# A bf16 softmax tail, a split last load and a 64-byte pad in a low-rank attention decode kernel

## The chip, the cores and the metric

One core of one Trainium2 chip. The metric is the device time of the whole program in microseconds (us), as the median of several runs. A profile (one execution recorded by the hardware profiler) has a span about 2 us shorter than the device time (330.8 against 332.58 before); it runs from the first instruction to the end of the last.

## The reference, cut to what matters

```python
B, H, Sq, Skv, Dh, R = 1, 16, 1, 8192, 256, 16     # all inputs bf16
kp = einsum("rn,bhnd->bhrd", e_proj, k)            # 8192 rows of K reduced to 16
vp = einsum("rn,bhnd->bhrd", f_proj, v)            # the same for V
scores = einsum("bhqd,bhrd->bhqr", q, kp) * Dh ** -0.5
p = softmax(scores)
o = einsum("bhqr,bhrd->bhqd", p, vp)
```

K and V are 16 heads x 8192 x 256 x 2 bytes each, 134.2 MB together, and every byte is used once. Everything after the two projections is tiny: 16 scores per head.

## The kernel before

The sync engine (SP) issues K and V in 64 transfers of 2 MB (half a head each), alternating, into five buffers of each. A transfer puts 16 KB in each of 128 partitions. For each chunk the tensor engine (PE) does 32 matmuls, one per slot of 128 rows, into four groups of 32 partitions of PSUM (the `psum_tensor` tiles that its matmuls write to). At the end of a head a "tail" adds the four groups and computes the attention:

```python
def T1(hh): ...   # kpT_ps <- kp_sb, S : add the four groups and transpose, 2 matmuls, fp32
def T2(hh): ...   # sc_ps  <- qT_sb, kpT_sb : 16 scores, 2 matmuls, fp32
def T3(hh):       # pT_ps  <- p_rep, S : the probabilities from a row to a column, fp32
    pe.wait_ge(sem_dve, dv_idx(hh, 4))
    ...
def T4(hh): ...   # o_ps   <- PT4, vp_sb : one row of the output, fp32
...
# where the tail stands in PE's order: the last head's T1, T2, T3 follow its last K chunk
if hh == H - 1:
    tgt = (2 * CH * H - 2) if t < 3 else (2 * CH * H - 1)
else:
    tgt = 2 * CH * (hh + 1) - 1 + t * step
```

Between T2 and T3, the vector engine (DVE) takes the maximum and scales it, the scalar engine (ACT) takes the exponential and its sum, and DVE takes the reciprocal and writes the normalised row four times (`p_rep`):

```python
dv.reciprocal(rs_sb[0:1, 0:1], sum_sb[0:1, 0:1]).then_inc(sem_dv2, 1)
...
for g in range(G):
    ins = dv.tensor_scalar(p_rep[0:1, 32 * g:32 * g + R], e_sb[0:1, 0:R],
                           rs_sb[0:1, 0:1], None, ALU.mult)
```

In the last head the matmuls of the last V chunk stand behind T3 in PE's program, and T3 waits for the whole softmax. The trace before has PE take them in that order: T3 began at 324.42 us, when `p_rep` was written, and the V matmuls at 324.88, though their data had landed at 323.33.

## Time and profile before

332.76 us, median of 4 runs (332.58 to 332.86).

The page of the profile, cut to some of its parts: the span; the busy time of the engines; the DMA strip in tenths of 40 equal slices; queues with packets, MB and share; the chain that ended last; the load of K with us from issue to landing. q1 carries K and V; q8, "instruction" on the page, is read as the program being fetched (17 packets here, 9 in the kernel of section 5 that has about half the PE instructions). PEld is PE's loading of weights, SPq is SP issuing a transfer.

```profile
span 330.8 us, 4863 instructions
PE 159.2 (48%) x2244; PEld 103.3 (31%) x2244; DVE 40.5 (12%) x181; ACT 7.0 (2%) x33; POOL 8.9 (3%) x18
...
DMA  8999999999999999999999999999999999999960
...
q1 hardware_dynamic: 9248, 134.23, 96.1%
...
q8 instruction: 17, 0.28, 0.3%
...
DMA 89%; PE 7%; issue 2%; DVE 1%; POOL 0%; ACT 0%; ACTq 0%; DVEq 0%; POOLq 0%
...
kbuf<-in_k_dram SPq DMA_DIRECT2D x32, 2048.0 KB, 47.0
```

The kernel is bound by the DMA: at nine tenths from the second slice to the 38th of 40, no engine above half. A transfer takes 47.0 us from issue to landing, and one lands every 4.9 us in the landing records, so about ten are queued (estimate: 47.0 / 4.9). A wait of PE or DVE in the middle did not stop the stream: PE waited 149.4 us for K and V in all (72.2 and 77.2 on the page), and the strip stays at nine tenths. So the two places where time can be saved are the stream itself and the drain, which is the work left after the last data has landed.

The timeline of the drain (start us, duration us, engine, line, operation, what it writes and reads, count; in brackets how long the engine was idle, and for what):

```profile
318.49 1.90 PE L323 MATMUL kp_acc<-kbuf,Wk 128*32 128x256 bf16 x32 [2.37 <-DMA kbuf<-in_k_dram]
...
321.16 1.04 PE L245 MATMUL kpT_ps<-S,kp_sb 112*128 112x16 f32 x4
...
322.48 0.26 PE L258 MATMUL sc_ps<-kpT_sb,qT_sb 128*1 128x16 f32 x4 [0.28 <-DVE kpT_sb L361]
...
323.73 0.64 DVE L377 TENSOR_SCALAR p_rep<-e_sb,rs_sb 1x16 f32<-1x16 f32 x4
...
324.42 0.53 PE L269 MATMUL pT_ps<-S,p_rep 1*112 1x1 f32 x2 [1.68 <-DVE p_rep L377]
...
324.88 1.90 PE L323 MATMUL vp_acc<-vbuf,Wv 128*32 128x256 bf16 x32
326.90 0.42 DVE L388 COPY vp_sb<-vp_acc 128x256 f32<-128x256 f32 x1 [2.53 <-PE vp_acc L323]
...
327.44 1.03 PE L279 MATMUL o_ps<-vp_sb,PT 112*16 112x256 f32 x2 [0.67 <-DVE PT L392]
328.51 0.41 DVE L396 CAST out_sb<-o_ps 16x256 bf16<-16x256 f32 x1 [1.12 <-PE o_ps L279]
328.95 0.36 SPq L204 DMA_DIRECT2D out_dram<-out_sb  x1
```

The V matmuls start at 324.88, and the bracket that a DMA wait would leave is missing: they came straight after pT. The chunk they read had landed 1.5 us earlier. That can't be seen in this view; it is in the landing records of the trace. Each of the 64 transfers of K and V has sixteen of them. The page reckons with 16 DMA engines, so I read them as one per engine, here and below; the records do not name the engine. The sixteen of the last V chunk, in us from the start of the span:

```
318.75 318.77 318.88 318.89 318.90 318.99 319.07 320.98 321.97 321.99 322.01 322.14 322.16 322.19 322.20 323.33
```

Seven engines are done at 318.9, seven at 322.1, one in between, and one, alone, at 323.33. The program waits for all sixteen, so the transfer counts as landed at 323.33.

### The profile page before, as it was taken

To read this page: it belongs to the slowest core of one execution; us is meant where nothing else is said; L and a number is where in the kernel's file an instruction comes from. 1 tells how busy PE (TensorE), PEld (TensorE's weight loads), DVE (VectorE), ACT (ScalarE), POOL (GpSimd) and SP (SyncE) were. 2 spreads that over 40 slices of the span, in tenths; PEclk is the share of its full clock that TensorE was granted. 3 is DMA by queue.
4 is the path that set the end of the run, shared out by engine and by line. 5 is a ranking of instruction groups with operands and counts; after the bars stand their busy time and mean duration, and the time that the engine had idled before them with its cause. 6 is when DMAs were issued, how large, how long until landed. Compare 5 with 4: busy or idle time off the path is not lost.

```text
span 330.8 us, 4863 instructions
## 1 busy us (share of the span) xinstructions
PE 159.2 (48%) x2244; PEld 103.3 (31%) x2244; DVE 40.5 (12%) x181; ACT 7.0 (2%) x33; POOL 8.9 (3%) x18
## 2 busy tenths in 40 slices
PE   0164364455446455455445445455355446536364
PEld 0143242243233324233223233334233233324242
DVE  0420101010010100101010010100101010010102
ACT  1000000000000000000000000000000000000000
POOL 8200000000000000000000000000000000000000
PEclk9996555555555555555555555555555555555555
DMA  8999999999999999999999999999999999999960
GB/s 284 384 428 426 428 424 432 420 434 420 434 422 434 420 433 424 428 428 424 432 420 436 418 434 420 434 424 430 424 428 426 426 428 426 426 430 424 428 292 1
DMA packets 9459, 135.07 MB, mean 408 GB/s; under 512 B 1088, under 2 KB 1120, under 8 KB 1248
## 3 DMA queue, kind: packets, MB, share of 16 engines
q1 hardware_dynamic: 9248, 134.23, 96.1%
q0 software_dynamic: 192, 0.54, 0.5%
q8 instruction: 17, 0.28, 0.3%
q14 instruction: 2, 0.02, 0.0%
HBM read 134.75 MB, written 0.01 MB: 407 GB/s over the span
## 4 chain that ended last, share of the span: by engine, by line
DMA 89%; PE 7%; issue 2%; DVE 1%; POOL 0%; ACT 0%; ACTq 0%; DVEq 0%; POOLq 0%
DMA kbuf<-in_k_dram 86%; PE kp_acc L323 5%; DMA q_nat<-in_q_dram 3%; PE vp_acc L323 1%; PE o_ps L279 1%; POOL Wk_tmp L127 0%; PE kpT_ps L229 0%; PE kpT_ps L245 0%; DVE p_rep L377 0%; PE pT_ps L269 0%; DVE vp_sb L388 0%; DVE out_sb L396 0%; PE sc_ps L258 0%; ACT e_sb L214 0%; DVE kpT_sb L361 0%
## 5 line engine op out<-in xcount | busy, mean ns | idle before, releaser
L323 PE MATMUL kp_acc<-kbuf,Wk 128*32 128x256 bf16 x1024 | 60.7, 417 | 77.4 <-DMA kbuf<-in_k_dram 72.2
L323 PE MATMUL vp_acc<-vbuf,Wv 128*32 128x256 bf16 x1024 | 60.0, 413 | 77.2 <-DMA vbuf<-in_v_dram 77.2
L323 PEld LDWEIGHTS vp_acc<-vbuf,Wv 128*32 128x32 bf16 x1024 | 35.4, 138 | 101.8 <-DMA vbuf<-in_v_dram 92.1
L323 PEld LDWEIGHTS kp_acc<-kbuf,Wk 128*32 128x32 bf16 x1024 | 35.8, 139 | 90.2 <-DMA kbuf<-in_k_dram 75.1
L279 PE MATMUL o_ps<-vp_sb,PT 112*16 112x256 f32 x32 | 16.9, 633 | 0.7 <-DVE PT L392 0.7
L245 PEld LDWEIGHTS kpT_ps<-S,kp_sb 112*128 112x128 f32 x64 | 14.7, 320 | 6.8 <-issue 6.0
L245 PE MATMUL kpT_ps<-S,kp_sb 112*128 112x16 f32 x64 | 16.4, 377 | 0.0
L357 DVE COPY kp_sb<-kp_acc 128x256 f32<-128x256 f32 x16 | 6.8, 425 | 69.6 <-PE kp_acc L323 69.6
L361 DVE COPY kpT_sb<-kpT_ps 128x32 f32<-128x32 f32 x16 | 3.1, 192 | 80.7 <-PE kpT_ps L245 80.7
L214 ACT ACTIVATE e_sb<-sc_ps,nb_sb 1x16 f32<-1x16 f32 x16 | 4.3, 266 | 315.8 <-DVE nb_sb L369 315.8
L377 DVE TENSOR_SCALAR p_rep<-e_sb,rs_sb 1x16 f32<-1x16 f32 x64 | 10.2, 218 | 0.6
L365 DVE TENSOR_REDUCE m_sb<-sc_ps 1x1 f32<-1x16 f32 x16 | 2.6, 162 | 61.6 <-PE sc_ps L258 61.6
L269 PEld LDWEIGHTS pT_ps<-S,p_rep 1*112 1x112 f32 x32 | 7.1, 282 | 8.0 <-issue 6.2
L269 PE MATMUL pT_ps<-S,p_rep 1*112 1x1 f32 x32 | 8.5, 332 | 1.7 <-DVE p_rep L377 1.7
L392 DVE COPY PT<-pT_ps 112x1 f32<-112x1 f32 x16 | 2.5, 158 | 51.7 <-PE pT_ps L269 51.7
L229 PE MATMUL kpT_ps<-S,q_nat 16*128 16x16 f32 x4 | 1.0, 367 | 12.1 <-DMA q_nat<-in_q_dram 12.1
L388 DVE COPY vp_sb<-vp_acc 128x256 f32<-128x256 f32 x16 | 6.5, 406 | 2.5 <-PE vp_acc L323 2.5
L258 PEld LDWEIGHTS sc_ps<-kpT_sb,qT_sb 128*1 128x1 f32 x64 | 4.8, 104 | 2.5 <-DVE kpT_sb L361 0.4
L279 PEld LDWEIGHTS o_ps<-vp_sb,PT 112*16 112x16 f32 x32 | 4.6, 147 | 2.9 <-DVE PT L392 1.1
L258 PE MATMUL sc_ps<-kpT_sb,qT_sb 128*1 128x16 f32 x64 | 5.0, 199 | 0.3 <-DVE kpT_sb L361 0.3
L229 PEld LDWEIGHTS kpT_ps<-S,q_nat 16*128 16x128 f32 x4 | 0.9, 319 | 12.1 <-DVE S L342 12.1
L373 DVE RECIPROCAL rs_sb<-sum_sb 1x1 f32<-1x1 f32 x16 | 2.4, 151 | 6.8 <-ACT e_sb L214 6.8
(23 smaller groups left out, 21.1 us busy)
## 6 DMA issues: line engine op xcount, KB each, us to landing
kbuf<-in_k_dram SPq DMA_DIRECT2D x32, 2048.0 KB, 47.0
vbuf<-in_v_dram SPq DMA_DIRECT2D x32, 2048.0 KB, 47.0
Wk_tmp<-in_e_proj_dram POOLq DMA_DIRECT2D x1, 256.0 KB, 9.4
Wv_tmp<-in_f_proj_dram POOLq DMA_DIRECT2D x1, 256.0 KB, 12.8
q_nat<-in_q_dram POOLq DMA_DIRECT2D x1, 16.0 KB, 9.4
out_dram<-out_sb SPq DMA_DIRECT2D x1, 8.0 KB, 1.4
```

The lines of the kernel that those rows point to most:

```text
L214: act.activation(e_sb[0:1, 0:R], sc_ps[0:1, 0:R], ACTF.Exp, bias=nb_sb[0:1, 0:1], scale=SCALE, accum_out=sum_sb[0:1, 0:1],).then_inc(sem_a ...
L245: ins2 = pe.matmul(kpT_ps[0:P, c2 * R:(c2 + 1) * R], kp_sb[0:KP, c2 * P:(c2 + 1) * P], S[0:KP, 0:R], start=True, stop=True,)
L258: ins2 = pe.matmul(sc_ps[0:1, 0:R], qT_sb[0:P, c2 * H + hh:c2 * H + hh + 1], kpT_sb[0:P, c2 * R:(c2 + 1) * R], start=(c2 == 0), stop=(c2 = ...
L269: pe.matmul(pT_ps[0:KP, 0:1], p_rep[0:1, 0:KP], S[0:1, 0:1], start=True, stop=True,).then_inc(sem_pe_t, 1)
L279: pe.matmul(o_ps[0:16, 0:D], PT4[0:KP, 16 * hh:16 * hh + 16], vp_sb[0:KP, 0:D], start=(hh == 0), stop=(hh == H - 1),).then_inc(sem_pe_t, 1)
L323: ins = pe.matmul(acc[32 * g:32 * g + MW, 0:D], W[0:P, j, 0:MW], buf[0:P, s, 0:D], start=(j < G), stop=(j >= JT - G), tile_position=(0, 32 ...
L357: dv.tensor_copy(kp_sb[0:KA, 0:D], kp_acc[hh % 2][0:KA, 0:D]).then_inc(sem_dve, 1)
L361: dv.tensor_copy(kpT_sb[0:P, 0:2 * R], kpT_ps[0:P, 0:2 * R]).then_inc(sem_dve, 1)
L365: dv.tensor_reduce(m_sb[0:1, 0:1], sc_ps[0:1, 0:R], AX.X, ALU.max).then_inc(sem_dv2, 1)
L377: ins = dv.tensor_scalar(p_rep[0:1, 32 * g:32 * g + R], e_sb[0:1, 0:R], rs_sb[0:1, 0:1], None, ALU.mult,)
L388: dv.tensor_copy(vp_sb[0:KA, 0:D], vp_acc[hh % 2][0:KA, 0:D]).then_inc(sem_dve, 1)
L392: dv.tensor_copy(PT4[0:KP, 16 * hh + hh:16 * hh + hh + 1], pT_ps[0:KP, 0:1]).then_inc(sem_dve, 1)
```

## The change

The intent is to shorten the work behind the last K and V chunk. The tail becomes bf16, the normalisation moves from the 16 probabilities to the output (a column of ones in `vp_sb` yields the sum), exp writes its four copies itself, T3 of the last head moves behind the V matmuls, and the last V chunk comes in two transfers. A `pad` tile of 64 bytes is added ahead of the K and V buffers. The core of the diff:

```diff
-    NDV = 6
+    NDV = 5
...
-        kp_sb = ... [P, D], fp32        # also kpT_sb, qT_sb, S, PT4, e_sb
-        vp_sb = ... [P, D], fp32
+        kp_sb = ... [P, D], bf16
+        vp_sb = ... [P, D + 1], bf16
...
+        pad = ctx.enter_context(nc.sbuf_tensor("pad", [P, 16], fp32))
         kbufs = []
...
+                    elif c == NCH - 1 and SL >= 2:
+                        h1 = 3 * SL // 4
+                        eng.dma_start(vbufs[c % NB][:, 0:h1, :], src[:, 0:h1, :]).then_inc(sem_vdma[c % NB], 16)
+                        eng.dma_start(vbufs[c % NB][:, h1:SL, :], src[:, h1:SL, :]).then_inc(sem_vlast, 16)
...
-                        e_sb[0:1, 0:R], sc_ps[0:1, 0:R], ACTF.Exp, ..., accum_out=sum_sb[0:1, 0:1],
+                        e_sb[0:1, 0:G, 0:R], sc_ps[...].to_broadcast([1, G, R]), ACTF.Exp, ...
...
-                            tgt = (2 * CH * H - 2) if t < 3 else (2 * CH * H - 1)
+                            tgt = (2 * CH * H - 2) if t < 2 else (2 * CH * H - 1)
...
-                    dv.reciprocal(rs_sb ...)            # and the four p_rep scalings, per head
...
-                dv.tensor_copy(out_sb[0:H, 0:D], o_ps[0:H, 0:D])
+                dv.reciprocal(rs_all[0:16, 0:1], o_ps[0:16, D:D + 1])
+                dv.tensor_scalar(out_sb[0:H, 0:D], o_ps[0:H, 0:D], rs_all[0:H, 0:1], float(G), ALU.mult, ALU.mult)
```

More of the change, by code (lines that the diff above doesn't have):

```diff
@@ L49, in bass_standalone__low_rank_proj_linformer__decode_kernel @@
     assert D <= 256 and 2 * max(H, R) <= 32
-    NDV = 6
-    POOL_TOTAL = 7 + G
+    NDV = 5
+    POOL_TOTAL = 9 + G
     W_CAST = (W_ENG == "pool")
@@ L57, in dv_idx @@
         return DV0 + NDV * h + step
-    DVE_FINAL = DV0 + NDV * H + 1
+    DVE_FINAL = DV0 + NDV * H + 2
     def pt_idx(h, t):
@@ L77, in bass_standalone__low_rank_proj_linformer__decode_kernel @@
         sem_out = ctx.enter_context(nc.semaphore("sem_out"))
+        sem_vlast = ctx.enter_context(nc.semaphore("sem_vlast"))
         Wk = ctx.enter_context(nc.sbuf_tensor("Wk", [P, JT, MW], bf16))
@@ L81, in bass_standalone__low_rank_proj_linformer__decode_kernel @@
         Wv_tmp = ctx.enter_context(nc.sbuf_tensor("Wv_tmp", [P, R, JT], bf16))
-        kp_sb = ctx.enter_context(nc.sbuf_tensor("kp_sb", [P, D], fp32))
-        vp_sb = ctx.enter_context(nc.sbuf_tensor("vp_sb", [P, D], fp32))
-        kpT_sb = ctx.enter_context(nc.sbuf_tensor("kpT_sb", [P, 2 * R], fp32))
-        qT_sb = ctx.enter_context(nc.sbuf_tensor("qT_sb", [P, 2 * H], fp32))
-        S = ctx.enter_context(nc.sbuf_tensor("S", [P, R], fp32))
+        kp_sb = ctx.enter_context(nc.sbuf_tensor("kp_sb", [P, D], bf16))
+        vp_sb = ctx.enter_context(nc.sbuf_tensor("vp_sb", [P, D + 1], bf16))
+        kpT_sb = ctx.enter_context(nc.sbuf_tensor("kpT_sb", [P, 2 * R], bf16))
+        qT_sb = ctx.enter_context(nc.sbuf_tensor("qT_sb", [P, 2 * H], bf16))
+        S = ctx.enter_context(nc.sbuf_tensor("S", [P, R], bf16))
         q_dt = fp32 if W_CAST else bf16
@@ L89, in bass_standalone__low_rank_proj_linformer__decode_kernel @@
         S16 = ctx.enter_context(nc.sbuf_tensor("S16", [16, 16], q_dt))
-        e_sb = ctx.enter_context(nc.sbuf_tensor("e_sb", [1, R], fp32))
-        m_sb = ctx.enter_context(nc.sbuf_tensor("m_sb", [1, 1], fp32))
+        e_sb = ctx.enter_context(nc.sbuf_tensor("e_sb", [1, G, 32], bf16))
         nb_sb = ctx.enter_context(nc.sbuf_tensor("nb_sb", [1, 1], fp32))
-        sum_sb = ctx.enter_context(nc.sbuf_tensor("sum_sb", [1, 1], fp32))
-        rs_sb = ctx.enter_context(nc.sbuf_tensor("rs_sb", [1, 1], fp32))
-        p_rep = ctx.enter_context(nc.sbuf_tensor("p_rep", [1, P], fp32))
-        PT4 = ctx.enter_context(nc.sbuf_tensor("PT4", [P, H * 16], fp32))
+        rs_all = ctx.enter_context(nc.sbuf_tensor("rs_all", [16, 1], fp32))
+        PT4 = ctx.enter_context(nc.sbuf_tensor("PT4", [P, H * 16], bf16))
         out_sb = ctx.enter_context(nc.sbuf_tensor("out_sb", [H, D], bf16))
@@ L104, in bass_standalone__low_rank_proj_linformer__decode_kernel @@
         pT_ps = ctx.enter_context(nc.psum_tensor("pT_ps", [P, 1], fp32))
-        o_ps = ctx.enter_context(nc.psum_tensor("o_ps", [16, D], fp32))
+        o_ps = ctx.enter_context(nc.psum_tensor("o_ps", [16, D + 1], fp32))
+        pad = ctx.enter_context(nc.sbuf_tensor("pad", [P, 16], fp32))
         kbufs = []
@@ L146, in stream_dmas @@
                         )
+                    elif c == NCH - 1 and SL >= 2:
+                        h1 = 3 * SL // 4
+                        src = v_src(hh, ch)
+                        eng.dma_start(vbufs[c % NB][:, 0:h1, :], src[:, 0:h1, :]).then_inc(
+                            sem_vdma[c % NB], 16
+                        )
+                        eng.dma_start(vbufs[c % NB][:, h1:SL, :], src[:, h1:SL, :]).then_inc(
+                            sem_vlast, 16
+                        )
                     else:
@@ L177, in _ @@
                 gp.wait_ge(sem_pool, pc[0])
-                pstep(gp.memset(p_rep[:, :], 0.0))
+                pstep(gp.memset(vp_sb[0:KA, D:D + 1], 1.0))
+                gp.wait_ge(sem_pool, pc[0])
+                pstep(gp.memset(e_sb[:, :, :], 0.0))
+                gp.wait_ge(sem_pool, pc[0])
+                pstep(gp.memset(rs_all[:, :], 0.0))
                 gp.wait_ge(sem_pool, pc[0])
@@ L214, in _ @@
                     act.activation(
-                        e_sb[0:1, 0:R],
-                        sc_ps[0:1, 0:R],
+                        e_sb[0:1, 0:G, 0:R],
+                        sc_ps[0:1, 0:R].rearrange("p (g r) -> p g r", g=1).to_broadcast([1, G, R]),
                         ACTF.Exp,
                         bias=nb_sb[0:1, 0:1],
-                        scale=SCALE,
-                        accum_out=sum_sb[0:1, 0:1],
+                        scale=1.0,
                     ).then_inc(sem_act, 1)
@@ L267, in T3 @@
                 def T3(hh):
-                    pe.wait_ge(sem_dve, dv_idx(hh, 4))
-                    pe.matmul(
-                        pT_ps[0:KP, 0:1],
-                        p_rep[0:1, 0:KP],
+                    pe.wait_ge(sem_act, hh + 1)
+                    ins2 = pe.matmul(
+                        pT_ps[0:KA, 0:1],
+                        e_sb[0:1, :, :].rearrange("p g r -> p (g r)"),
                         S[0:1, 0:1],
@@ L274, in T3 @@
                         stop=True,
-                    ).then_inc(sem_pe_t, 1)
+                    )
+                    ins2.then_inc(sem_pe_t, 1)
                 def T4(hh):
-                    pe.wait_ge(sem_dve, dv_idx(hh, 6))
+                    pe.wait_ge(sem_dve, dv_idx(hh, 5))
                     pe.matmul(
-                        o_ps[0:16, 0:D],
+                        o_ps[0:16, 0:D + 1],
                         PT4[0:KP, 16 * hh:16 * hh + 16],
-                        vp_sb[0:KP, 0:D],
+                        vp_sb[0:KP, 0:D + 1],
                         start=(hh == 0),
@@ L317, in _ @@
                     if ch == 0 and hh >= 2:
-                        pe.wait_ge(sem_dve, dv_idx(hh - 2, 1 if pj == 0 else 5))
+                        pe.wait_ge(sem_dve, dv_idx(hh - 2, 1 if pj == 0 else 4))
                     ins = None
@@ L322, in _ @@
                         g = j % G
+                        if pj == 1 and c == NCH - 1 and SL >= 2 and s == 3 * SL // 4:
+                            pe.wait_ge(sem_vlast, 16)
                         ins = pe.matmul(
@@ L343, in _ @@
                 dv.wait_ge(sem_pe_t, 1)
-                dv.tensor_copy(qT_sb[0:P, 0:2 * H], kpT_ps[0:P, 0:2 * H]).then_inc(
-                    sem_dve, 1
-                )
+                dv.tensor_scalar(
+                    qT_sb[0:P, 0:2 * H], kpT_ps[0:P, 0:2 * H], SCALE, None, ALU.mult
+                ).then_inc(sem_dve, 1)
                 dv.wait_ge(sem_wk, 16)
@@ L365, in _ @@
                     dv.tensor_reduce(
-                        m_sb[0:1, 0:1], sc_ps[0:1, 0:R], AX.X, ALU.max
-                    ).then_inc(sem_dv2, 1)
-                    dv.wait_ge(sem_dv2, 2 * hh + 1)
-                    dv.tensor_scalar(
-                        nb_sb[0:1, 0:1], m_sb[0:1, 0:1], -SCALE, None, ALU.mult
-                    ).then_inc(sem_dve, 1)
-                    dv.wait_ge(sem_act, hh + 1)
-                    dv.reciprocal(rs_sb[0:1, 0:1], sum_sb[0:1, 0:1]).then_inc(sem_dv2, 1)
-                    dv.wait_ge(sem_dv2, 2 * hh + 2)
-                    ins = None
-                    for g in range(G):
-                        ins = dv.tensor_scalar(
-                            p_rep[0:1, 32 * g:32 * g + R],
-                            e_sb[0:1, 0:R],
-                            rs_sb[0:1, 0:1],
-                            None,
-                            ALU.mult,
-                        )
-                    ins.then_inc(sem_dve, 1)
+                        nb_sb[0:1, 0:1], sc_ps[0:1, 0:R], AX.X, ALU.max, negate=True
+                    ).then_inc(sem_dve, 1)
                     if hh >= 1:
@@ L395, in _ @@
                 dv.wait_ge(sem_pe_t, pt_idx(H - 1, 4))
-                dv.tensor_copy(out_sb[0:H, 0:D], o_ps[0:H, 0:D]).then_inc(sem_dve, 1)
+                dv.reciprocal(rs_all[0:16, 0:1], o_ps[0:16, D:D + 1]).then_inc(sem_dve, 1)
+                dv.wait_ge(sem_dve, DVE_FINAL - 1)
+                dv.tensor_scalar(
+                    out_sb[0:H, 0:D], o_ps[0:H, 0:D], rs_all[0:H, 0:1], float(G),
+                    ALU.mult, ALU.mult,
+                ).then_inc(sem_dve, 1)
 _INS = ['q', 'k', 'v', 'e_proj', 'f_proj']
```

## The prediction

> **What bounds it now.** The kernel reads 134.2 MB of K and V in 64 transfers of 2 MB. The 40-slice strip shows the DMA engines at 9 tenths from the second slice to the next to last, at about 427 GB/s; the chain of waits is 89% DMA. The page shows 47.0 us from issue to landing, so about ten transfers are always queued and no engine work in the middle holds the stream up. PE is busy 48% with a granted clock of 0.5, DVE 12%, ACT 2%. Work removed in the middle (heads 0 to 14) therefore saves nothing.
>
> What counts is the drain. In the timeline the last K chunk is waited for until 318.49 us. By the landing records of its semaphore the last V chunk lands at about 323.3 us (half of the engines are done at 318.8, most of the others at 322.0, one at 323.3). The span ends at 330.8. Its order: K matmuls 1.90, o_ps of head 14 0.84 more, kpT 1.0, copy 0.2, scores 0.28, max and bias 0.35, exp 0.27, reciprocal 0.16, four p_rep scalings 0.65, pT matmul 0.53, and only then (324.9) the V matmuls, 1.9, because PE runs in order and pT stands ahead of them. Then vp copy 0.42, PT 0.08, o_ps 1.05, cast 0.41, store about 1.9.
>
> **What changes there.**
> - PE no longer sits behind softmax: pT is moved behind the V matmuls. The fp32 matmuls become bf16; each fp32 one shows as two records now (o_ps 2 x 0.63 us overlapped into 1.05), so I estimate o_ps 0.4 (one 256-column bf16 matmul here shows 0.42), kpT 0.35. Scores should end near 321.6.
> - The last V chunk comes in 3/4 and 1/4. The slowest engine's last chunk takes 4.9 us from K's landing, so 3/4 should land near 322.1 and the rest at 323.3. V matmuls run from about 322.1 to 324.0 (now 324.9 to 326.8); max, exp run beside them.
> - Added at the end: pT after V (about 0.2, beside the 0.42 vp copy), PT copy 0.15 now exposed, reciprocal 0.15, and scaling instead of cast, about 0.41. o_ps falls by 0.65.
> Sum: 324.05 + 0.45 copy + 0.17 PT + 0.4 o_ps + 0.2 reciprocal + 0.45 scale + 1.9 store = about 327.6, or 3.2 us less. The extra Pool memsets at the start (some 0.1 to 0.3 us each) delay the first matmuls, which don't bind: ten transfers are queued.
>
> **The stream itself.** One side effect: smaller tiles plus the 64-byte `pad` move the K and V buffers. By the layout they start at 192 modulo 256 now and would start at 0 modulo 256 afterwards. [...] A 16 KB packet takes 613 ns here[...]
>
> **Time.** 329.1 us, range 326.2 to 330.3. Chances: faster by over 2% 0.15, within 2% 0.84, slower 0.01.
>
> **Signs.** Right: DMA still 9 everywhere, V matmuls of the last chunk starting near 322 with two DMA waits, about 4.3 us from last landing to end (7.5 now), 16 KB packets still 613 ns. Wrong: [...]last K landing moved by over 1 us; or pT waiting on exp behind V.
>
> **Risks.** The buffer move, the straggling DMA engine landing elsewhere, the split's second semaphore landing late.

The forecast's sum was 332.8 us less 3.2 for the drain less 0.5 for the moved buffers: 329.1 us. The 0.5 term was the author's guess.

## The result, and the profile after

326.15 us, median of 8 runs (325.96 to 326.27); before in the same rounds 332.86 us (13 runs). The ratio is 0.9798, with a 95% interval of 0.9789 to 0.9808. Ratios here are the mean time of one kernel's fast runs over that of the other's of the same rounds, so they are not quite the ratio of the quoted medians. The interval reaches over 0.98, so whether the gain is more than 2% is left unclear. The gain is 6.7 us; the prediction had 3.7.

The page after, the same parts (span, engines, DMA strip, queues, chain):

```profile
span 324.2 us, 4563 instructions
PE 129.6 (40%) x2148; PEld 81.4 (25%) x2148; DVE 26.2 (8%) x86; ACT 6.2 (2%) x17; POOL 9.1 (3%) x20
...
DMA  7999999999999999999999999999999999999992
...
q1 hardware_dynamic: 9392, 134.23, 97.4%
...
q8 instruction: 17, 0.28, 0.3%
...
DMA 94%; PE 4%; SPq 0%; DVE 0%; issue 0%
```

The timeline of the drain after:

```profile
315.07 1.90 PE L337 MATMUL kp_acc<-kbuf,Wk 128*32 128x256 bf16 x32 [2.83 <-DMA kbuf<-in_k_dram]
...
317.50 0.22 PE L256 MATMUL kpT_ps<-S,kp_sb 112*128 112x16 bf16 x2 [0.33 <-DVE kp_sb L371]
...
318.01 0.20 PE L269 MATMUL sc_ps<-kpT_sb,qT_sb 128*1 128x16 bf16 x2 [0.28 <-DVE kpT_sb L375]
...
318.44 0.30 ACT L226 ACTIVATE e_sb<-sc_ps,nb_sb 1x64 bf16<-1x64 f32 x1 [10.59 <-DVE nb_sb L379]
...
318.72 1.90 PE L337 MATMUL vp_acc<-vbuf,Wv 128*32 128x256 bf16 x32 [0.51 <-DMA vbuf<-in_v_dram]
319.95 0.18 PEld L337 LDWEIGHTS vp_acc<-vbuf,Wv 128*32 128x32 bf16 x8 [0.25 <-DMA vbuf<-in_v_dram]
...
320.55 0.18 PE L280 MATMUL pT_ps<-S,e_sb 1*128 1x1 bf16 x1
320.73 0.42 DVE L385 CAST vp_sb<-vp_acc 128x256 bf16<-128x256 f32 x1 [2.33 <-PE pT_ps L280]
...
321.28 0.38 PE L291 MATMUL o_ps<-vp_sb,PT 112*16 112x257 bf16 x1 [0.55 <-DVE PT L389]
321.70 0.16 DVE L393 RECIPROCAL rs_all<-o_ps 16x1 f32<-16x1 f32 x1 [0.47 <-PE o_ps L291]
321.89 0.47 DVE L395 TENSOR_SCALAR out_sb<-o_ps,rs_all 16x256 bf16<-16x256 f32 x1
322.39 0.36 SPq L216 DMA_DIRECT2D out_dram<-out_sb  x1
```

Two things are to be seen. V now waits twice for DMA (at 318.72 for three quarters, at 319.95 for the rest) and no longer for the softmax. And the last K chunk is taken up at 315.07 instead of 318.49: the stream before the drain, which the change was not about, is 3.4 us shorter.

All data of the last V chunk has landed at 323.33 before and at 319.91 after. So the 6.56 us between the two spans divide into

- the stream, up to the last landing: 323.33 - 319.91 = 3.42 us;
- the drain, from the last landing to the end: 7.47 before and 4.33 after, 3.14 us.

The drain is what the prediction said ("about 4.3 us from last landing to end (7.5 now)"). The stream is where the other half came from. The landing records of the last transfer (the last quarter of V), after:

```
316.58 316.67 316.75 316.80 316.83 316.88 316.98 317.68 319.66 319.69 319.72 319.83 319.84 319.86 319.88 319.91
```

The early half moved from 318.9 to 316.8, the late half from 322.1 to 319.8, and the one engine that came alone at 323.33 is gone. These are two different effects: some 2.1 to 2.3 us for everybody, and 1.1 us for the straggler. The next section takes them apart.

The packets of K and V in the two traces (durations of the 16 KB packets in ns, with how many took that long; the change has fewer of 16 KB because the last V chunk has smaller ones):

```
before: 611 x476, 612 x710, 613 x4122, 614 x223, 615 x144, 616 x43, 618 x467, 620 x1644, 621 x73 ...   mean of those under 700 ns: 615.1
after:  611 x7768, 612 x14, 614 x18, 615 x14 ...                                             mean of those under 700 ns: 611.5
```

3.65 ns x 512 packets per DMA engine (8192 packets over 16 engines) = 1.9 us. The packets themselves became faster and uniform.

### The profile page after: what moved, and what is told of

Its sections match the earlier page's. It is cut to its first block, busy times and chain, and to the rows that moved or that the text cites. A ratio compares the mean times of both kernels' runs of the same rounds, so it can differ in the third digit from the quotient of the medians.

```text
span 324.2 us, 4563 instructions
## 1 busy us (share of the span) xinstructions
PE 129.6 (40%) x2148; PEld 81.4 (25%) x2148; DVE 26.2 (8%) x86; ACT 6.2 (2%) x17; POOL 9.1 (3%) x20
## 4 chain that ended last, share of the span: by engine, by line
DMA 94%; PE 4%; SPq 0%; DVE 0%; issue 0%
DMA vbuf<-in_v_dram 94%; PE vp_acc L337 4%; SPq L143 0%; DVE out_sb L395 0%; DVE vp_sb L385 0%; SPq L156 0%; PE o_ps L291 0%; DVE rs_all L393 0%; PE pT_ps L280 0%; DVE PT L389 0%
## 5 line engine op out<-in xcount | busy, mean ns | idle before, releaser
L371 DVE CAST kp_sb<-kp_acc 128x256 bf16<-128x256 f32 x16 | 6.8, 425 | 74.6 <-PE kp_acc L337 74.6
L226 ACT ACTIVATE e_sb<-sc_ps,nb_sb 1x64 bf16<-1x64 f32 x16 | 4.9, 305 | 311.8 <-DVE nb_sb L379 311.8
L375 DVE CAST kpT_sb<-kpT_ps 128x32 bf16<-128x32 f32 x16 | 3.1, 192 | 66.8 <-PE kpT_ps L256 66.8
L379 DVE TENSOR_REDUCE nb_sb<-sc_ps 1x1 f32<-1x16 f32 x16 | 2.6, 163 | 71.0 <-PE sc_ps L269 71.0
L291 PE MATMUL o_ps<-vp_sb,PT 112*16 112x257 bf16 x16 | 6.7, 420 | 0.6 <-DVE PT L389 0.6
L385 DVE CAST vp_sb<-vp_acc 128x256 bf16<-128x256 f32 x16 | 6.6, 413 | 2.7 <-PE pT_ps L280 2.3
L269 PEld LDWEIGHTS sc_ps<-kpT_sb,qT_sb 128*1 128x1 bf16 x32 | 3.9, 125 | 2.5 <-DVE kpT_sb L375 0.4
L269 PE MATMUL sc_ps<-kpT_sb,qT_sb 128*1 128x16 bf16 x32 | 3.9, 195 | 0.3 <-DVE kpT_sb L375 0.3
L256 PE MATMUL kpT_ps<-S,kp_sb 112*128 112x16 bf16 x32 | 3.5, 184 | 0.3 <-DVE kp_sb L371 0.3
L280 PE MATMUL pT_ps<-S,e_sb 1*128 1x1 bf16 x16 | 2.9, 180 | 0.0
```

The source lines that it names most:

```text
L226: act.activation(e_sb[0:1, 0:G, 0:R], sc_ps[0:1, 0:R].rearrange("p (g r) -> p g r", g=1).to_broadcast([1, G, R]), ACTF.Exp, bias=nb_sb[0:1 ...
L256: ins2 = pe.matmul(kpT_ps[0:P, c2 * R:(c2 + 1) * R], kp_sb[0:KP, c2 * P:(c2 + 1) * P], S[0:KP, 0:R], start=True, stop=True,)
L269: ins2 = pe.matmul(sc_ps[0:1, 0:R], qT_sb[0:P, c2 * H + hh:c2 * H + hh + 1], kpT_sb[0:P, c2 * R:(c2 + 1) * R], start=(c2 == 0), stop=(c2 = ...
L280: ins2 = pe.matmul(pT_ps[0:KA, 0:1], e_sb[0:1, :, :].rearrange("p g r -> p (g r)"), S[0:1, 0:1], start=True, stop=True,)
L291: pe.matmul(o_ps[0:16, 0:D + 1], PT4[0:KP, 16 * hh:16 * hh + 16], vp_sb[0:KP, 0:D + 1], start=(hh == 0), stop=(hh == H - 1),).then_inc(sem ...
L371: dv.tensor_copy(kp_sb[0:KA, 0:D], kp_acc[hh % 2][0:KA, 0:D]).then_inc(sem_dve, 1)
```

## The experiments

The theory after the result: (a) the drain gain is the shorter chain and the split; (b) the packets are faster because the K and V buffers start at a multiple of 256 bytes (192 modulo 256 before, 0 after, by the layout of the program); (c) the straggler went because the PE program is shorter and its last instruction fetch falls later. The rival to (b) and (c): the stream is faster because the engines do lighter work. For (c) the page has the first hint: q8 moved 17 packets of 16 KB, of the kind "instruction". In the kernel after, PE executed 201 to 270 instructions between two of them (256 on average), and one such packet took 0.89 to 1.27 us.

The table sums up what the traces of all runs say. It is worked out from packet and landing records: mean of the 16 KB packets of K and V under 700 ns, number of fetches, start of the last fetch, landing of the last V data in the early half (median of the first 7 engines), in the late half (median of the 9th to 15th) and of the last engine, and the drain from there to the end.

```
kernel                        time us  packet ns  fetches  last fetch  early   late    last    drain
before                        332.86   615.1      17       311.6       318.9   322.1   323.33  7.47
after                         326.15   611.5      17       319.7       316.8   319.8   319.91  4.33
before + pad                  330.54   611.4      17       309.3       316.8   319.6   321.43  7.53
after, no pad (offset 192)    328.54   615.1      17       322.0       318.9   322.1   322.29  4.31
after, offset 64              328.55   615.1      17       322.1       318.9   322.0   322.16  4.31
after, offset 128             328.43   614.9      17       322.1       318.9   321.8   322.17  4.32
after, V not split            327.19   611.5      17       320.9       316.7   319.6   319.90  5.57
after, pT before V            326.33   611.5      17       319.7       316.8   319.7   319.87  4.56
before, pT behind V           331.41   615.1      17       312.0       318.9   322.0   323.73  6.01
after, tail in fp32           328.61   611.4      17       309.6       316.6   319.7   321.16  5.55
after, PE instructions added  327.64   611.4      17       309.2       316.7   319.6   321.34  4.34
after, two slots per matmul   326.04   611.5       9       312.5       316.8   318.2   319.78  4.34
the same, fewer (wrong)       324.64   611.4       8       308.5       316.8   318.2   318.41  4.36
```

### 1. The pad alone, and the change without it

```diff
 (kernel before)
+        pad = ctx.enter_context(nc.sbuf_tensor("pad", [P, 16], fp32))
         kbufs = []
```
```diff
 (kernel after)
-        pad = ctx.enter_context(nc.sbuf_tensor("pad", [P, 16], fp32))
```

> The kernel before with one unused 64-byte tile in front of the K and V buffers, so that they start at 0 instead of 192 modulo 256; every instruction is as before. Alignment theory: 16 KB packets take 611 ns throughout (before: 613, with 620 in about 29 percent of them), about 2.0 us come off the stream, and the straggling engine at the last landing stays, because the instruction stream is unchanged: about 330.7 us. If alignment is the whole stream gain: about 329.4 us. Rival (the stream got shorter through the lighter bf16 engine work or fewer instructions): packets stay at 613 and 620 ns and the time stays at 332.8 us.

> The changed kernel without its pad tile: K and V buffers start at 192 modulo 256 again, as in the kernel before. Alignment theory: packets back at 613 and 620 ns, about 2.0 us more, 328.2 us. If alignment was the whole stream gain of 3.4 us: 329.5 us. Rival (lighter engine work): stays at 326.2 us with 611 ns packets.

Measured: 330.54 us (before in the same rounds 332.93, ratio 0.9931, interval 0.9916 to 0.9946), and 328.54 us (ratio 0.9870, interval 0.9853 to 0.9886). The pad is worth 2.39 us on the kernel before and 2.39 us on the kernel after. Not one instruction differs in the first pair, and packets go from 615.1 to 611.4 ns on average. In the second pair they go back to 615.1 although all engine work is the lighter kind. The rival is out for this part. In the padded kernel before one engine still lands alone (321.43 against a late half at 319.6): alignment did not remove the straggler. Of the 2.39 us, 1.9 are the packets under 700 ns. In the first pair the traces leave no rest: their spans differ by 1.85 us (330.80 and 328.95; the executions profiled were the fastest of the kernel before and the slowest of the padded one). In the second pair the spans differ by 2.36 us. A part of that rest is in the program fetches of section 5: with the slow packet behind it, one takes 1.56 us of an engine's time at offset 192 and 1.43 when aligned (medians). What is left beyond that was not looked into.

### 2. Is it the distance from 256 bytes?

```diff
-        pad = ctx.enter_context(nc.sbuf_tensor("pad", [P, 16], fp32))
+        pad = ctx.enter_context(nc.sbuf_tensor("pad", [P, 32], fp32))     # buffers at 64 modulo 256; [P, 48]: at 128
```

> The changed kernel with the buffers starting at 64 modulo 256. [...] If any misalignment to 256 costs the same: 328.2 us. If only 64-byte alignment matters: 326.2 us.

> The changed kernel with the buffers starting at 128 modulo 256. [...] If any misalignment to 256 costs the same: 328.2 us. If 128-byte alignment is what matters: 326.2 us and 611 ns.

Measured: 328.55 us at offset 64 and 328.43 us at offset 128, against 328.54 at 192 and 326.15 at 0. A buffer off by 64, 128 or 192 bytes costs the same, 2.3 to 2.4 us, and the packets take 614.9 to 615.1 ns at all three, against 611.5. The cost does not grow with the offset here. Smaller offsets were not tried.

### 3. The parts of the drain

The last V chunk in one transfer, with the rest of the change as it is:

```diff
-                    elif c == NCH - 1 and SL >= 2:
+                    elif False:
...
-                        if pj == 1 and c == NCH - 1 and SL >= 2 and s == 3 * SL // 4:
+                        if False:
```

> The changed kernel with the last V chunk in one transfer, as before. The last landing stays at 319.9 us in the trace; the 32 V matmuls can then start only there, and their 1.9 us stand whole behind it, instead of ending at 320.6: about 1.2 us more, 327.4 us. Rival (the split is worth nothing, because PE or the exp is what V waits for): 326.2 us.

Measured: 327.19 us (327.05 to 328.32), 1.04 us more. In its timeline the V matmuls start when everything has landed (319.90), and the store is issued 1.23 us later than in the kernel after:

```profile
319.95 1.90 PE L337 MATMUL vp_acc<-vbuf,Wv 128*32 128x256 bf16 x32 [1.68 <-DMA vbuf<-in_v_dram]
...
323.62 0.36 SPq L216 DMA_DIRECT2D out_dram<-out_sb  x1
```

The order of pT, put back in the kernel after, and changed alone in the kernel before:

```diff
 (kernel after)
-                            tgt = (2 * CH * H - 2) if t < 2 else (2 * CH * H - 1)
+                            tgt = (2 * CH * H - 2) if t < 3 else (2 * CH * H - 1)
```
```diff
 (kernel before)
-                            tgt = (2 * CH * H - 2) if t < 3 else (2 * CH * H - 1)
+                            tgt = (2 * CH * H - 2) if t < 2 else (2 * CH * H - 1)
```

> The changed kernel with pT of the last head ahead of the V matmuls in PE's order, as before. In the changed kernel exp ends at 318.74 us and V begins at 318.72, so pT would be in the way for only 0.2 us: 326.3 us. Rival (the order is a main part of the gain in the drain, as the prediction had it first in its list): 327.5 us or more.

> The kernel before with only the order changed: pT of the last head after the V matmuls. V should start when its chunk lands (323.4 us in the trace) instead of at 324.9, and pT and the PT copy then stand behind it: about 1.4 us less, 331.4 us. If the order is worth as little here as it should be in the changed kernel: 332.7 us.

Measured: 326.33 us (0.18 more than after, hardly beyond the spread of the runs, but the drain in its trace is 0.23 longer) and 331.41 us (1.4 less than before, 332.82 in the same rounds). The same edit is worth 1.4 us in one kernel and 0.2 in the other, because in the kernel after exp ends (318.74) just as V's data comes (318.72): the parts of the drain overlap, and their values can't be added. The moved normalisation and exp's four copies were not tested alone. In the kernel before with only the order changed, the bracket of the missing DMA wait appears:

```profile
323.77 1.90 PE L323 MATMUL vp_acc<-vbuf,Wv 128*32 128x256 bf16 x32 [0.62 <-DMA vbuf<-in_v_dram]
```

The small tiles and the tail matmuls in fp32 again, in the kernel after (the pad made larger so that the buffers stay at 0 modulo 256):

```diff
-        kp_sb = ... bf16      # and vp_sb, kpT_sb, qT_sb, S, e_sb, PT4
+        kp_sb = ... fp32
-        pad = ctx.enter_context(nc.sbuf_tensor("pad", [P, 16], fp32))
+        pad = ctx.enter_context(nc.sbuf_tensor("pad", [P, 40], fp32))
```

> The changed kernel with its small tiles and tail matmuls in fp32 again (buffers still at 0 modulo 256). The drain gets longer by o_ps 0.65, pT 0.35 and the V matmuls starting about 0.9 later, about 1.9 us; and the PE program again has the 12 more instructions per head, so an engine of the DMA should again straggle by about 1.1 us at the last landing. Together about 329.0 us; with the drain alone (no straggler): 328.0 us.

Measured: 328.61 us, 2.46 more. The table divides it: the last engine lands 1.25 us later (321.16), again alone, and the drain is 1.22 us longer (5.55). The drain part is smaller than the 1.9 expected: the straggler makes the last K chunk late too (taken up at 316.36), and V, which now waits for the scores and not for its data, starts 4.03 us after it, against 3.65 in the kernel after. The slower scores cost 0.4 and not 0.9. Each fp32 tail matmul stands in the trace as two, as in the kernel before; that is the link to the next experiment.

### 4. The straggler: as many PE instructions as before, without fp32

```diff
-                    for c2 in range(2):                                         # T1, the same in T2
+                    for c2 in (range(2) if hh == H - 1 else (0, 1, 0, 1)):
...
+                    for _rep in range(1 if hh == H - 1 else 3):                 # around the matmul of T3
```

> The changed kernel, with six of the bf16 tail matmuls of each head but the last simply repeated (same operands, same result), so that PE has as many instructions per head as in the kernel before (12 more). Instruction-fetch theory: the 17th 16 KB instruction fetch, which came at the very end in the changed kernel, comes back some 10 us before the end, one DMA engine gets a third one and lands its last share 1.1 to 1.5 us after all others: 327.4 us, with 611 ns packets and an unchanged drain of 4.3 us. Rival (the straggler came from fp32 or from the old buffer addresses): 326.2 us and no straggler.

Measured: 327.64 us, 1.49 more than after, with 611.4 ns packets and a drain of 4.34. Repeating 90 tiny matmuls whose own time is hidden behind the loads costs 1.5 us. The DMA view of the stretch from 307 to 318 us shows the reason. First the kernel before, then the kernel after, then this one (packets, MB, share of 16 engines; the share is lower in the last two because seven of their engines are done by 317 us):

```profile
q1 hardware_dynamic: 317, 4.62, 99.3%
q8 instruction: 1, 0.02, 0.6%
```

```profile
q1 hardware_dynamic: 386, 4.34, 92.6%
```

```profile
q1 hardware_dynamic: 388, 4.30, 92.0%
q8 instruction: 1, 0.02, 0.5%
```

The kernels with the long PE program fetch their 17th packet at 309 to 312 us, while data is still being moved; the short one fetches it at 319.7, when the data is practically there. And the last V data then lands at

```
with PE instructions added: 316.54 316.56 316.63 316.66 316.68 316.88 316.94 317.50 319.49 319.51 319.55 319.60 319.63 319.72 319.79 321.34
```

which is the list of the kernel after with one engine 1.55 us behind the others.

### 5. Where the two halves come from, and a shorter program

The landing lists of the kernel after can be read from its start to its end: how many of the sixteen engines land late in a transfer, against the median of the five earliest, and how many 16 KB program packets (q8) had begun by then.

```
transfer landed at (us)        9    32   51   70   90   109  129  148  168  189  208  227  247  266  286  305  320
program packets by then        0    1    2    3    4    5    6    7    8    9    10   11   12   14   15   16   17
engines over 1.1 us late       0    1    2    3    4    5    6    7    8    8    8    8    8    8    8    8    8
of them over 2.2 us late       0    0    0    0    0    0    0    0    0    1    2    3    4    5    6    7    8
```

By these counts one more engine is late after each fetch (for the first the slowest landing is 1.7 us behind the median at 32 us, for the ninth 3.2 us at 174 us, so about 1.5 us a fetch), and it stays behind to the end of the stream. The lateness falls on eight of the sixteen, once each with the first eight fetches and a second time with the next eight; the other eight are never over 1.1 us late. A fetch that began less than a microsecond before the landing does not show yet: the 14th, 15th and 16th in the columns of 266, 286 and 305 us, and the 17th, which began at 319.7 us and was too late to matter. So the late half, 3.0 us behind, is read as eight engines with two fetches each.

The packets show what the 1.5 us consist of, though their records name no engine. From 1 to 16 ns before each fetch ends, one 16 KB data packet begins that takes 1.07 to 1.16 us instead of 0.61. It is so for all 17 fetches of the kernel before and for 16 of the 17 of the kernel after, and in the other runs too, except for the last fetch of the kernels that fetch it as the data ends (319.7 us or later). In the kernels before and after no other 16 KB packet later than 16 us takes over 0.66 us, but for those behind q14 packets, named under what stays open. The fetch takes 0.88 to 1.11 us; with what the packet takes beyond 611 ns that is 1.42 to 1.58 us. And the durations of the slow packets repeat after eight fetches (kernel after, ns, in order of time):

```
1079 1079 1089 1158 1158 1102 1107 1114
1079 1079 1091 1158 1158 1102 1106 1115
```

The test is a kernel with half the PE instructions, two slots per matmul for all heads but the last:

```diff
-                    for s in range(SL): ...
+                    if hh < H - 1:
+                        for s in range(0, SL, 2):
+                            j = ch * SL + s
+                            g = (j // 2) % 2
+                            ins = pe.matmul(acc[64 * g:64 * g + 64, 0:2 * D],          # 64 x 512, diagonal blocks used
+                                W[0:P, j:j + 2, 0:MW].rearrange("p a r -> p (a r)"),
+                                buf[0:P, s:s + 2, 0:D].rearrange("p a d -> p (a d)"),
+                                start=(j < 4), stop=(j >= JT - 4), tile_position=(0, 64 * g), ...)
... (PSUM accumulators [P, 2 * D]; kp_sb and vp_sb evicted in four copies of 32 partitions)
```

> The changed kernel with two slots of a chunk per matmul for all heads but the last: 64 weight columns and 512 moving columns, of which the diagonal blocks are used, evicted in four copies. PE has about half the instructions. Instruction-fetch theory: about 9 fetches in place of 17; eight DMA engines that now end 3.0 us late (two fetches of about 1.5 us each) end 1.5 us late, so the stream ends 1.5 us sooner: 324.6 us (326.1 if the ninth still falls before the end). [...] Rival (the late half of the DMA engines is late for another reason than instruction fetches): 326.2 us with the same 3.0 us gap.

Measured: 326.04 us, correct, no better than the kernel after (ratios to before 0.9793 and 0.9798). PE takes 3.26 us for such a chunk (V at 298.92 us in its timeline), less than the 4.9 us between two landings in the kernel after. Its page (engines, queue of the program):

```profile
PE 181.9 (56%) x1188; PEld 74.7 (23%) x1188; DVE 63.9 (20%) x176; ACT 6.2 (2%) x17; POOL 9.1 (3%) x20
...
q8 instruction: 9, 0.15, 0.2%
```

The time alone would have been taken for "no effect". The landings say otherwise: the late half is now only 1.4 us behind the early one (318.2 against 316.8; 3.0 in the kernel after), and a single engine lands at 319.78. By the same count as above, eight engines are over 1.1 us late and one of them over 2.2: nine fetches fit one for each of eight engines and a second for one. It was foreseen as the second case in the expectation. To see what the ninth alone costs, the program was shortened further by leaving work out; the result is wrong.

```diff
-                        for s in range(0, SL, 2):
+                        for s in range(0, SL - 8 if ch == 0 and hh < H - 2 else SL, 2):
```

> WRONG RESULT ON PURPOSE, to size one thing: the two-slots-per-matmul kernel with the last 4 of 16 matmuls left out in the first chunk of K and of V of heads 0 to 13 (112 matmuls and weight loads fewer, all loads of K and V as before). PE waits for DMA anyway, so its work itself is worth nothing. Instruction-fetch theory: PE's program is some 220 instructions shorter, so the ninth fetch no longer falls before the end; no engine straggles, the last landing comes about 1.5 us sooner (at 318.3 us) and the time is 324.5 us. Rival (the straggler or the late half has another cause): 326.0 us, as the kernel with all its matmuls.

Measured: 324.64 us (ratio 0.9751, interval 0.9735 to 0.9768), last landing 318.41, eight fetches (queue of the program, from its page):

```profile
q8 instruction: 8, 0.13, 0.1%
```

So the theory's number came out again: with the ninth fetch inside the stream (at 312.5 us) the time is 1.4 us longer than with eight. One late engine is enough for that, as the program waits for all sixteen. A correct kernel at 324.6 us would need about 110 PE instructions fewer ahead of its last V chunk than the two-slots kernel has (estimate from the instruction counts in the traces: the last V chunk begins after about 2340 PE instructions, the ninth fetch came after 2266 here and after 2230 in the kernel after). That wasn't built, so no correct version here clearly beats the kernel after.

What stays open: why only eight of the sixteen landings are late after the fetches, which engines they belong to, and why the data packet behind a fetch takes half a microsecond longer (1.07 to 1.16 us against 0.61). One engine of the early half lands 0.8 to 2.1 us after the others of its half in every run. This goes with 8 KB packets of another program queue (q14), each with a data packet of 1.14 to 1.27 us behind it (1.27 at 117.6 and at 315.0 us before, 1.15 at 214.1 us after): the three runs with two of them inside the stream (before, before + pad, before with pT behind V) have 1.8 to 2.1 us, those with one 0.8 to 1.4. No run was made to test it, as that engine is never the last. What a packet does with a start off 256 bytes, and why some of them (28% in the kernel before) then take 618 to 622 ns, is not shown either.

## Why the prediction was right or wrong

- **What bounds the kernel, and the drain: right.** The chain of waits and the landing records gave 7.5 us from last landing to end, and 4.3 was predicted; 7.47 and 4.33 were measured. Its parts hold in the timeline: o_ps 0.38 (0.4 predicted), scaling 0.47 (0.45), two DMA waits in front of V 1.2 us apart. The exception is kpT, 0.22 against 0.35, which was harmless. The order of pT, which the prediction lists first, turned out to be worth only 0.2 us beside the other parts; its sum does not suffer, as it counts from the landings.
- **"Work removed in the middle (heads 0 to 14) therefore saves nothing": this step failed.** It holds for busy time (with two slots per matmul PE is busy 181.9 us in place of 129.6, and the time is 326.04 us against 326.15). It does not hold for the number of instructions: the fetches of PE's program run among the data packets, and each left one engine about 1.5 us late (section 5). With 12 PE instructions fewer per head, the last fetch came at 319.7 us in place of 311.6 and no longer fell inside the stream, and the straggler went: 1.1 us by the landing records, 1.5 us when it was brought back. The prediction read the straggler (its landing at 323.3) and took it as a given; under the risks it said only that it might land elsewhere.
- **The moved buffers: named, the weight was wrong.** The prediction saw that the buffers would move and added half a microsecond for it, a guess. Packets went from 615.1 to 611.5 ns on average, and the pad was worth 2.39 us on either kernel. What makes a packet slower at another start is not shown.
- **The sum.** 3.2 for the drain (3.14 measured), 0.5 for the stream (3.42 measured). So the term that failed is the stream, by both steps above: some 2.3 us are the moved buffers, 1.1 the straggler. Either alone would have left the time inside the range (estimate: with 2.4 in place of the 0.5, 327.2; with 1.1 for the straggler besides, 326.1). The 326.15 us lies just under the range's lower end of 326.2, and "within 2%" was given 0.84 where the ratio came out at 0.9798, on the border.
- **The sign it gave for being wrong, "last K landing moved by over 1 us", did show:** the last K chunk was taken up 3.4 us sooner. Of its signs for being right, "16 KB packets still 613 ns" failed: most took 611.

## What to carry to other kernels

In a kernel bound by DMA, look at the landing of each DMA engine in the last transfers, not only at the mean rate: the program waits for all sixteen landings of a transfer, and here eight of them came 3 us behind the others after 16 fetches of PE's program. Count the fetches of the program as DMA traffic (here one packet of 16 KB for 256 PE instructions on average), and ask whether one falls just before the end: at 309.2 us the 17th cost 1.5 us, at 319.7 us it did not show. And check where large DMA buffers start: here 0 modulo 256 bytes was 2.3 to 2.4 us better than 64, 128 or 192 (no other load pattern was tried). A change of small tiles can move them, as it did here, and then a change that seems to be about compute speeds up or slows down the packets (615.1 ns at 192, 611.5 at 0).
